# Spreading the weights' sums over a half, moving half of the operand rests to VectorE, and respacing the attention steps in a fused attention and FFN kernel

## The chip, the core and the metric

One core of a Trainium2 chip runs the kernel. The metric is the device time of one execution in microseconds (us). The time before is the median of three runs, 850.99 us (850.49 to 851.1). Five engines run side by side, each through its own instructions in program order: TensorE (PE; its weight loads are PEld), VectorE (DVE), ScalarE (ACT), GpSimd (POOL) and SyncE (SP), whose queue issues nearly all DMAs here.

## What is computed

Attention within chunks of 64 tokens (8 heads of 64 features), then a normalization, a feed-forward layer with ReLU, and the residual, all in fp32:

```python
scores = scale * np.matmul(q_c, k_c.transpose(0, 1, 2, 4, 3))   # chunks of 64 tokens
attn = np.exp(scores - np.max(scores, axis=-1, keepdims=True))
attn = attn / (np.sum(attn, axis=-1, keepdims=True) + 1e-09)
x = np.matmul(attn, v_c)                        # as (8 * 576 tokens, 512)
xn = (x - mean(x)) / np.sqrt(var(x) + 1e-06) * g_ln
out = x + np.maximum(xn @ w_ch1, 0.0) @ w_ch2   # 512 -> 2048 -> 512
```

## The kernel before

The 4608 tokens are 18 pairs of 128 (256 tokens each). To keep fp32 accuracy, every operand of the FFN is split in a high part (rounded on ScalarE, fp32r) and a rest (operand minus high part, on VectorE or GpSimd), and every product is three: high x high, high x rest, rest x high.

The first three tiles (six pairs) run in `START`, `SECOND` and `THIRD`, with an order written out by letters. They take the first 325 us of the profile, and the change does not touch them. The other 12 pairs are three **units** of four pairs (1024 tokens), `unit_ffn(u)` for u = 0, 1, 2. A unit has two stages:

- *Up*: the product with the first weights, in four quarters q. Seven products of sums of blocks take the place of eight products of blocks, so that a quarter has 14 steps of 6 matmuls (named "2", "1", "6", "5", "7", "3", "4"; L965). ScalarE copies banks out (L971), VectorE adds them (L974) into the tiles `h0` to `h7` (`hu`, L953 to L956; each holds two halves n of the tokens, two blocks f and 512 columns). The "4" product of a quarter goes into a bank that VectorE has first to read by the addition after "7".
- *Down*: for units 0 and 1, two halves n of 512 tokens, each 16 blocks f of 12 matmuls (L1092). Block f needs its high part (`split`, ScalarE, L1010) and its rest (`rest`, VectorE, L1015), which are issued two blocks ahead: the rest of block f + 2 after the eighth matmul of block f, and it is used from the eighth matmul of block f + 2 on, 24 matmuls later. Unit 2 (`tail`) has its own down stage (`double`, L891) in seven products as well; for this it needs sums of the second weights, in DRAM as `wb`.

Weights come through a ring of six places (`Ring`). After each block or each two up steps one more load is issued on SP's queue (L707 to L711).

Three things are done beside the matmuls of units 0 and 1:

- *Attention of the next unit's four pairs* (`following(u + 1, n)`), a generator of 20 steps: loads, scores (L302), maximum (L309), subtraction (L334), exp on ScalarE (L337), four steps of four transposes on VectorE (L362), row sums (L369), outputs (L391), scaling to x (L425), statistics (L435), xg (L447), its scaling on ScalarE (L453), one turn (L458), four steps of 4 row DMAs (L466).
- *`combine(u + 1, half)`*: the operands of the next unit's up stage from the rows of pairs 0 and 1 (half 0) or 2 and 3 (half 1): seven parts, each a high part on ScalarE (L773) and a rest on GpSimd (L774), and four subtractions on VectorE (L777).
- *`mix_weights(u)`*: for four p, the sums for `wb`: two sums of 512 columns out of the ring (L928), four of 256 (L935), a high part on ScalarE (L938), a rest on VectorE (L940), two DMAs (L942, L943). It is woven in by hand in the down stage of half n = 1: p = 0 to 3 in blocks 0 to 7 of unit 0, p = 4 to 7 in blocks 8 to 15 of unit 1. Its two buffers are the tiles `h0` and `h1`, in turn.

All is put in program order by `weave`: `unit_ffn` yields a cost, the number of its 512-column matmuls, and `side` is a list of (position, generator); a step is issued when the sum of the costs has come to its position. A unit has 720 positions: up 0 to 336, half n = 0 336 to 528, half n = 1 528 to 720. Pair n begins at position 114 n + 8, and its steps follow at the offsets of `STEPS`, scores at the first; `combine` has 11 steps, 9 positions apart, from 345 (half 0) and 515 (half 1). Steps are issued at the first yield at or after their position (every 6 positions in the up stage, every 4 in the blocks), and those with the same position in the order of the list.

Of the kernel before, what the change touches and what calls it, by code (L numbers as in the profile page):

```python
# [8 lines left out]
F32 = mybir.dt.float32  # L9
# [40 lines left out]

PAIR_SPAN = 114
LOADED = 8
STEPS = (0, 5, 9, 13, 18, 26, 34, 42, 50, 56, 62, 67, 76, 81, 87, 95, 104, 113, 122)
ONE_STEP = 9
FIRST_HALF = 345
LAST_HALF = 515
REST = (2, 6, 20)


# [41 lines left out]
def chunk_attention_ffn(ctx: ExitStack, tc: tile.TileContext, qkv, v01, g, w, out):  # L101
# [586 lines left out]
    class Ring:  # L688
# [22 lines left out]
                    nc.sync.dma_start(to.rearrange("p (h n) -> p h n", h=2), of)  # L711
                self.given += 1

        def peek(self, n):
            assert self.taken + n < self.given
            return self.places[(self.taken + n) % RING]

        def take(self):
            assert self.taken < self.given
# [35 lines left out]
    def operand(name):  # L755
        if name not in shared:
            shared[name] = const.tile([P, 2, 2, 2 * PAIR], F32R, name="xc", tag=f"w{'2165734'.index(name)}")
        return shared[name]

    def combine(u, half):  # L760
        cs = slice(half * PAIR, (half + 1) * PAIR)
        if u > 0:
            a, b = (
                r[:, half].rearrange("p j k t -> p (j k t)").rearrange("p (j k t) -> p k j t", k=NK, t=32)
                for r in shared["rows"]
            )
        else:
            a, b = (r[:, half].rearrange("p j k t -> p k j t") for r in shared["rows"])
        b11, b21, b12, b22 = a[:, :2], a[:, 2:], b[:, :2], b[:, 2:]

        def part(name, x):
            o = operand(name)[:, :, :, cs].rearrange("p h k (j t) -> p h k j t", t=32 if u > 0 else P)
            nc.scalar.copy(o[:, 0], x)  # L773
            nc.gpsimd.tensor_tensor(out=o[:, 1], in0=x, in1=o[:, 0].bitcast(F32), op=ALU.subtract)  # L774

        def less(out, x, y):
            nc.vector.tensor_tensor(out=out, in0=x, in1=y, op=ALU.subtract)  # L777

        part("2", b21)
        yield  # L780
        part("1", b11)
        yield
        less(b11, b12, b11)
        yield
        less(b12, b22, b12)
        yield
        part("3", b22)
        yield
        less(b22, b22, b11)
        yield  # L790
        part("6", b22)
        yield
        part("5", b11)
        yield
        less(b21, b21, b22)
        yield
        part("7", b12)
        yield
        part("4", b21)
        yield  # L800

    class double:

# [113 lines left out]
                    yield 3.17  # L917
                    self.advance(t + (k + 1) / 2)

    def mix_weights(u):  # L920
        for i in range(4):
            p = 4 * u + i
            space = shared[f"h{i % 2}"].rearrange("p n f d -> p (n f d)")
            t_ = space[:, : 2 * DM].rearrange("p (f d) -> p f d", f=2)
            his = space[:, 2 * DM :].bitcast(F32R).rearrange("p (f d) -> p f d", f=2)
            for k in range(2):
                w = ring.peek(k)[:, : 2 * DM].rearrange("p (h n) -> p h n", h=2).bitcast(F32)
                nc.vector.tensor_tensor(out=t_[:, k], in0=w[:, 0], in1=w[:, 1], op=ALU.add)  # L928
            yield
            b11, b12, b21, b22 = (t_[:, k // 2, k % 2 * PAIR : (k % 2 + 1) * PAIR] for k in range(4))  # L930
            for out, x, y, op in (
                (b11, b12, b11, ALU.subtract), (b12, b22, b12, ALU.subtract), (b22, b11, b22, ALU.subtract),
                (b21, b21, b22, ALU.add),
            ):
                nc.vector.tensor_tensor(out=out, in0=x, in1=y, op=op)  # L935
            yield
            yield
            nc.scalar.copy(his, t_)  # L938
            yield
            nc.vector.tensor_tensor(out=t_.bitcast(F32R), in0=t_, in1=his.bitcast(F32), op=ALU.subtract)  # L940
            yield
            nc.sync.dma_start(wb[:, p, 0], his.rearrange("p f (a n) -> p (f a) n", a=2).bitcast(F32))  # L942
            nc.sync.dma_start(wb[:, p, 1], t_.rearrange("p f (a n) -> p (f a) n", a=2))  # L943
            yield

    def unit_ffn(u):
        first = 2 * LEAD + 4 * u
# [138 lines left out]
        for n in range(2):  # L1086
            ys = [ps_y.tile([P, DM], F32, name="y") for _ in range(4 - 2 * n)]
            ys += [ps_h.tile([P, DM], F32, name="h") for _ in range(2 * n)]

            def down(f, w, j, m):  # L1090
                hh, hl = (x[:, j * P : (j + 1) * P] for x in parts[n * NF + f][:2])
                nc.tensor.matmul(  # L1092
                    ys[j], lhsT=(hh, hh, hl)[m], rhs=w[:, (0, 1, 0)[m]],
                    start=f == 0 and m == 0, stop=f == NF - 1 and m == 2,
                )

            pairs = [first + 2 * n, first + 2 * n + 1]
            early, late = ((2, 3, 0), 1) if n else ((0, 2, 1), 3)
            firsts = [(m, j) for m in range(2) for j in early] + [(0, late), (1, late)] + [(2, j) for j in (*early, late)]
            ws = {}  # L1100
            mixing = mix_weights(u) if n else iter(())
            for f in range(NF):
                if n and f >= 8 * u:
                    next(mixing, None)
                ws[f] = ring.take()[:, : 2 * DM].rearrange("p (h n) -> p h n", h=2)
                if f < NF - 2:
                    i = n * NF + f + ahead
                    for at, (m, j) in enumerate(
                        firsts if f == 0 else
                        [(m, j) for m in range(3) for j in range(4)]  # L1110
                    ):
                        down(f, ws[f], j, m)
                        if at % 4 == 3:
                            yield 4
                            if at == 11 and n == 0 and f == NF - 3:
                                split(NF)
                            if at == 3 and f > 0 and i - 1 < 2 * NF:
                                split(i - 1)
                            if at == 7 and f > 0 and i - 1 < 2 * NF:
                                rest(i - 1)  # L1120
                            if n and at < 8 and f >= 8 * u:
                                next(mixing, None)
                    ring.fetch()
                    if f == 6:
                        for pair in pairs:
                            back[pair] = unspill(pair)
                    for to, of in stores:
                        nc.sync.dma_start(to, of)
                    stores.clear()
            for j in range(4):  # L1130
                for f in range(NF - 2, NF):
                    for m in range(3):
                        down(f, ws[f], j, m)
                yield 6
                pair, jj = pairs[j // 2], j % 2
                x = back[pair][:, jj, :]
                nc.vector.tensor_tensor(out=x, in0=ys[j], in1=x, op=ALU.add)
                row = pair * PAIR + jj * P
                if tail and n == 1:
                    nc.sync.dma_start(out[row : row + P, :], x)  # L1140
                else:
                    stores.append((out[row : row + P, :], x))
                next(mixing, None)
# [54 lines left out]
    with tc.manual_schedule():  # L1198
# [19 lines left out]
        for u in range(UNITS):  # L1218
            side = [(at, now["Q"]) for at in REST] if u == 0 else []
            if u + 1 < UNITS:  # L1220
                for n in range(4):
                    begin = n * PAIR_SPAN + LOADED
                    side += [(begin + at, following(u + 1, n)) for at in STEPS]
                    side.append((begin + STEPS[0], following(u + 1, n + 1)))
                for half, begin in enumerate((FIRST_HALF, LAST_HALF)):
                    stream = combine(u + 1, half)
                    side += [(begin + i * ONE_STEP, stream) for i in range(11)]
            weave(unit_ffn(u), side)


# [33 lines left out]
```

## Time and profile before

| what | us |
|---|---|
| median of three runs | 850.99 |
| profiled execution, its time | 848.26 |
| profiled execution, its span (first to last instruction) | 846.5 |
| first part (tiles 0 to 2), from the chain | 0 to 324.75 |
| unit 0 (up 324.75 to 409.55, down to 507.59) | 182.84 |
| unit 1 (down from 592.39, to 686.03) | 178.44 |
| unit 2 (up to 762.19, down to 842.83) | 156.80 |

The starts are those of the merged pieces of the chain that ended last. Units 0 and 1 have the same matmuls. In the profile's groups a row reads: line, engine, operation, output <- inputs by the program's names, shape, count | busy us, mean ns of one | idle us of the engine before them, and what ended it. In the order of time: start, duration, engine, line, operation, count, and in brackets the idle time before it with what ended it. Instructions in a row on one engine are merged there.

### The profile page before, as it was taken

The numbers are of one execution on the slowest core, as the hardware profiler recorded it, in microseconds if no ns is written. First come the engines' busy times: TensorE is split into PE (matmuls) and PEld (weight loads), VectorE is DVE, ScalarE is ACT, GpSimd is POOL, SyncE is SP. The second block draws the span as 40 slices with busy tenths as digits, with TensorE's granted clock in tenths as the row PEclk, the third lists the DMA queues.
The fourth block names the chain that finished last, engine by engine and source line by source line (L and its number), as shares of the span: only waits on it lengthen the run. The fifth ranks groups of instructions, "written<-read, shape, count | busy, mean of one in ns | idle before, by whom it ended". The sixth has DMA issues, their size and how long they took to land.

```text
span 846.5 us, 15569 instructions
## 1 busy us (share of the span) xinstructions
PE 828.6 (98%) x6138; PEld 693.2 (82%) x6138; DVE 585.9 (69%) x961; ACT 298.3 (35%) x465; POOL 149.7 (18%) x138
## 2 busy tenths in 40 slices
PE   7999999999999999999999899999999999999998
PEld 4888888888888888878878688788788888889998
DVE  6999956777556736787795937679766653249854
ACT  5776432123331333232432312324333223245432
POOL 0110006474741133000231300000314000000000
PEclk9999999999999999999999999999999999999999
DMA  9997508937981138697787979778658897668672
GB/s 361 333 289 201 197 3 289 335 134 278 326 288 61 38 147 301 191 307 270 230 299 247 361 232 315 231 257 312 225 203 293 296 351 229 197 193 281 204 220 102
DMA packets 93113, 203.69 MB, mean 241 GB/s; under 512 B 9200, under 2 KB 47600, under 8 KB 91120
## 3 DMA queue, kind: packets, MB, share of 16 engines
q1 hardware_dynamic: 91744, 197.97, 67.7%
q0 software_dynamic: 1296, 4.72, 2.8%
q8 instruction: 49, 0.80, 0.4%
q14 instruction: 24, 0.20, 0.1%
HBM read 144.98 MB, written 48.76 MB: 229 GB/s over the span
## 4 chain that ended last, share of the span: by engine, by line
PE 90%; DVE 7%; DMA 1%; issue 1%; ACT 0%; SPq 0%; DVEq 0%
PE y L965 26%; PE h L547 16%; PE y L571 16%; PE y L1092 11%; PE y L891 10%; PE h L1092 4%; DVE pt_sb L362 2%; PE s L302 2%; PE h L391 1%; DVE hu L928 1%; DVE hx L1015 1%; PE s L391 1%; DMA k_t<-qkv 1%; DVE hu L935 1%; PE s L351 1%
## 5 line engine op out<-in xcount | busy, mean ns | idle before, releaser
L965 PE MATMUL y<-xc,ring 128*128 128x512 f32 x1008 | 233.2, 391 | 0.8 <-DVE hu L974 0.8
L965 PEld LDWEIGHTS y<-xc,ring 128*128 128x128 f32 x1008 | 188.2, 188 | 41.1 <-DVE hu L974 1.6
L547 PE MATMUL h<-xth,wp 128*128 128x512 f32 (+1 forms) x432 | 129.3, 370 | 0.0
L974 DVE TENSOR_TENSOR hu<-y,snap 128x512 f32<-128x512 f32 x72 | 49.1, 684 | 68.2 <-ACT snap L971 34.8
L571 PE MATMUL y<-wp,hh 128*128 128x512 f32 x376 | 96.2, 394 | 0.0
L547 PEld LDWEIGHTS h<-xth,wp 128*128 128x128 f32 x432 | 78.3, 188 | 14.0 <-DVE hl L561 0.2
L1092 PE MATMUL y<-ring,hx 128*128 128x512 f32 x324 | 84.5, 390 | 3.6 <-DVE hx L1015 3.6
L774 POOL TENSOR_TENSOR xc<-rows,xc 128x512 fp32r<-128x512 f32 x42 | 57.2, 1372 | 135.9 <-ACT xc L773 119.7
L362 DVE STREAM_TRANSPOSE pt_sb<-p_sb 32x256 f32<-32x256 f32 x176 | 76.7, 436 | 6.1 <-ACT p_sb L337 3.3
L571 PEld LDWEIGHTS y<-wp,hh 128*128 128x128 f32 x376 | 69.1, 188 | 13.9
L561 DVE SCALAR_TENSOR_TENSOR hl<-h,hh 128x512 fp32r<-128x512 f32 (+1 forms) x53 | 33.1, 629 | 65.4 <-ACT hh L560 65.1
L547 PE MATMUL h<-xtl,wp 128*128 128x512 f32 (+1 forms) x216 | 78.3, 367 | 0.0
L971 ACT COPY snap<-y 128x512 f32<-128x512 f32 x72 | 41.9, 585 | 101.5 <-PE y L965 101.3
L1092 PEld LDWEIGHTS y<-ring,hx 128*128 128x128 f32 x324 | 60.6, 188 | 17.1 <-DVE hx L1015 4.4
L560 ACT ACTIVATE hh<-h 128x512 fp32r<-128x512 f32 (+1 forms) x53 | 28.6, 546 | 117.7 <-PE h L547 117.7
L891 PE MATMUL y<-ring,hx 128*128 128x256 f32 x480 | 59.1, 283 | 0.0
L891 PEld LDWEIGHTS y<-ring,hx 128*128 128x128 f32 x480 | 58.2, 192 | 0.0
L571 PE MATMUL y<-wp,hl 128*128 128x512 f32 x188 | 51.8, 389 | 0.0
L1092 PE MATMUL y<-ring,hh 128*128 128x512 f32 x168 | 49.0, 407 | 0.0
L441 POOL TENSOR_TENSOR rstd<-vare,mhalf 128x2 f32<-128x2 f32 x12 | 10.5, 876 | 213.0 <-DVE vare L440 213.0
L547 PEld LDWEIGHTS h<-xtl,wp 128*128 128x128 f32 x216 | 40.3, 188 | 6.6 <-ACT xtl L510 0.2
L571 PEld LDWEIGHTS y<-wp,hl 128*128 128x128 f32 x188 | 35.3, 188 | 7.4
(153 smaller groups left out, 1149.9 us busy)
## 6 DMA issues: line engine op xcount, KB each, us to landing
ring<-wa SPq DMA_DIRECT2D x84, 512.0 KB, 4.5
ring<-w2d SPq DMA_DIRECT2D x64, 512.0 KB, 4.8
raw<-w SPq DMA_DIRECT2D x15, 1024.0 KB, 8.1
q_t<-qkv SPq DMA_DIRECT2D x17, 512.0 KB, 5.7
k_t<-qkv SPq DMA_DIRECT2D x17, 512.0 KB, 6.5
v_t<-qkv SPq DMA_DIRECT2D x32, 256.0 KB, 5.4
w2d<-wp SPq DMA_DIRECT2D x16, 512.0 KB, 7.6
wa<-parts SPq DMA_DIRECT2D x32, 256.0 KB, 4.6
```

Of the source, the lines that this page charges most:

```text
L302: nc.tensor.matmul(s[h2][c * D : (c + 1) * D, j * HP + a, :], lhsT=q_t[r, a, cs], rhs=k_t[r, a, cs], start=not den_by_pe or j == a == 0, s ...
L362: nc.vector.transpose(out=pt_sb[quad(2 * h2 + j), :, c, quad(i)], in_=p_sb[quad(2 * c + i), :, h2, quad(j)])
L547: nc.tensor.matmul(h, lhsT=(wh, wh, wl)[m][:, ks], rhs=(xth, xtl, xth)[m][:, k, :], start=i == 0, stop=i == len(terms) - 1,)
L560: nc.scalar.activation(hh, h, AF.Relu)
L561: nc.vector.scalar_tensor_tensor(out=hl, in0=h, scalar=0.0, in1=hh.bitcast(F32), op0=ALU.max, op1=ALU.subtract)
L571: nc.tensor.matmul(sums(pairs[j // 2])[j % 2], lhsT=(hh, hh, hl)[m], rhs=(wh, wl, wh)[m], start=f == 0 and m == 0, stop=f == NF - 1 and m ...
L774: nc.gpsimd.tensor_tensor(out=o[:, 1], in0=x, in1=o[:, 0].bitcast(F32), op=ALU.subtract)
L891: nc.tensor.matmul(bank[j // 2][:, j % 2 * PAIR : (j % 2 + 1) * PAIR], lhsT=(hh, hh, hl)[m][:, j * P : (j + 1) * P], rhs=loaded[t // 2][:, ...
L965: nc.tensor.matmul(bank, lhsT=w[:, (0, 0, 1)[m], ks], rhs=x[:, (0, 1, 0)[m], k, :], start=start and k == m == 0, stop=k == 1 and m == 2, s ...
L971: nc.scalar.copy(out, bank)
L974: nc.vector.tensor_tensor(out=out, in0=bank, in1=s, op=ALU.add)
L1092: nc.tensor.matmul(ys[j], lhsT=(hh, hh, hl)[m], rhs=w[:, (0, 1, 0)[m]], start=f == 0 and m == 0, stop=f == NF - 1 and m == 2,)
```

## The change

- `mix_weights(u, i)` takes one p of four at a time, in side steps: for i = 0 to 3, eight steps at 528 + 48 i + `MIXING`, so that one p falls to every four blocks of half n = 1, in both units. Unit u takes p = 2 i + u, whose weights are blocks 4 i + 2 u and 4 i + 2 u + 1 of the half. It reads them out of the ring by number (`ring.at`), in unit 1 two and three blocks ahead of the block under way. Its buffers are the n = 0 halves of `h{2i}` and `h{2i + 1}`, other ones for each i. The rest of 1024 columns becomes two of 512.
- `combine` of units 1 and 2 has 13 steps, and a rest is issued one or more steps after its high part. The rests of half 1 are on VectorE; those of half 0 stay on GpSimd. Half 0 runs from 426 with 8 positions between steps, half 1 from 562 with 12.
- `STEPS` has new offsets: the transposes are 11 positions apart (8 before), the outputs 67 behind the scores (56 before), with the later steps behind them. Pair 2 (n = 2) has its own offsets, `ACROSS`: xg and all that follows come 25 positions later than in `STEPS`, so that nothing of the pair falls between positions 313 and 346.

The order for unit 0's own operands (`combine(0, ...)`) keeps its 11 steps. The diff, without the deletion of the old loop's hooks in `unit_ffn` (`next(mixing, None)` in four places) and without the old list of `combine`, whose order stays in the `else` branch:

```diff
-STEPS = (0, 5, 9, 13, 18, 26, 34, 42, 50, 56, 62, 67, 76, 81, 87, 95, 104, 113, 122)
-ONE_STEP = 9
-FIRST_HALF = 345
-LAST_HALF = 515
+STEPS = (0, 5, 9, 14, 20, 31, 42, 53, 61, 67, 72, 77, 85, 90, 97, 104, 111, 118, 125)
+ACROSS = (0, 5, 9, 14, 20, 31, 42, 53, 61, 67, 72, 77, 110, 116, 123, 130, 136, 142, 148)
+HALVES = ((426, 8), (562, 12))
+SECOND_HALF = 528
+MIXING = (1, 4, 13, 16, 24, 37, 41, 47)
...
-        def peek(self, n):
-            assert self.taken + n < self.given
-            return self.places[(self.taken + n) % RING]
+        def at(self, i):
+            assert self.taken - 1 <= i < self.given
+            return self.places[i % RING]
...
+        engine = nc.vector if u > 0 and half == 1 else nc.gpsimd
+
+        def cast(name, x):
+            nc.scalar.copy(place(name)[:, 0], x)
+
+        def low(name, x):
+            o = place(name)
+            engine.tensor_tensor(out=o[:, 1], in0=x, in1=o[:, 0].bitcast(F32), op=ALU.subtract)
...
+        if u > 0:
+            steps = [
+                [(cast, "2", b21)], [(low, "2", b21), (cast, "1", b11)], [(low, "1", b11), (cast, "3", b22)],
+                [(less, b11, b12, b11)], [(low, "3", b22)], [(less, b12, b22, b12)], [(less, b22, b22, b11)],
+                [(cast, "6", b22), (cast, "5", b11)], [(low, "6", b22)], [(less, b21, b21, b22), (cast, "7", b12)],
+                [(low, "5", b11)], [(cast, "4", b21), (low, "7", b12)], [(low, "4", b21)],
+            ]
...
-    def mix_weights(u):
-        for i in range(4):
-            p = 4 * u + i
-            space = shared[f"h{i % 2}"].rearrange("p n f d -> p (n f d)")
-            t_ = space[:, : 2 * DM].rearrange("p (f d) -> p f d", f=2)
-            his = space[:, 2 * DM :].bitcast(F32R).rearrange("p (f d) -> p f d", f=2)
...
+    def mix_weights(u, i):
+        p = 2 * i + u
+        t_ = shared[f"h{2 * i}"][:, 0]
+        his = shared[f"h{2 * i + 1}"][:, 0].bitcast(F32R)
+        for k in range(2):
+            w = ring.at(ring.passed + 2 * p + k)[:, : 2 * DM].rearrange("p (h n) -> p h n", h=2).bitcast(F32)
+            nc.vector.tensor_tensor(out=t_[:, k], in0=w[:, 0], in1=w[:, 1], op=ALU.add)
+            yield
...
+            nc.vector.tensor_tensor(out=out, in0=x, in1=y, op=op)
+            if k % 2:
+                yield
+        nc.scalar.copy(his, t_)
+        yield
+        for k in range(2):
+            nc.vector.tensor_tensor(
+                out=t_[:, k].bitcast(F32R), in0=t_[:, k], in1=his[:, k].bitcast(F32), op=ALU.subtract
+            )
+            yield
+        nc.sync.dma_start(wb[:, p, 0], his.rearrange("p f (a n) -> p (f a) n", a=2).bitcast(F32))
+        nc.sync.dma_start(wb[:, p, 1], t_.rearrange("p f (a n) -> p (f a) n", a=2))
+        yield
...
-                    side += [(begin + at, following(u + 1, n)) for at in STEPS]
+                    side += [(begin + at, following(u + 1, n)) for at in (ACROSS if n == 2 else STEPS)]
                     side.append((begin + STEPS[0], following(u + 1, n + 1)))
-                for half, begin in enumerate((FIRST_HALF, LAST_HALF)):
+                for half, (begin, step) in enumerate(HALVES):
                     stream = combine(u + 1, half)
-                    side += [(begin + i * ONE_STEP, stream) for i in range(11)]
+                    side += [(begin + i * step, stream) for i in range(13)]
+                for i in range(NF // 4):
+                    stream = mix_weights(u, i)
+                    side += [(SECOND_HALF + 12 * i * 4 + at, stream) for at in MIXING]
```

More of the change, by code (lines that the diff above doesn't have):

```diff
@@ L769, in combine, with place, part @@
         b11, b21, b12, b22 = a[:, :2], a[:, 2:], b[:, :2], b[:, 2:]
[L771 to L774, printed above, removed]
+        def place(name):
+            return operand(name)[:, :, :, cs].rearrange("p h k (j t) -> p h k j t", t=32 if u > 0 else P)
+        engine = nc.vector if u > 0 and half == 1 else nc.gpsimd
[4 more added lines that the diff above has]
+            engine.tensor_tensor(out=o[:, 1], in0=x, in1=o[:, 0].bitcast(F32), op=ALU.subtract)
         def less(out, x, y):
             nc.vector.tensor_tensor(out=out, in0=x, in1=y, op=ALU.subtract)
[L779 to L800, printed above, removed]
+        def part(name, x):
+            cast(name, x)
+            low(name, x)
+        if u > 0:
[5 more added lines that the diff above has]
+            ]
+        else:
+            steps = [
+                [(part, "2", b21)], [(part, "1", b11)], [(less, b11, b12, b11)], [(less, b12, b22, b12)],
+                [(part, "3", b22)], [(less, b22, b22, b11)], [(part, "6", b22)], [(part, "5", b11)],
+                [(less, b21, b21, b22)], [(part, "7", b12)], [(part, "4", b21)],
+            ]
+        for step in steps:
+            for what, *args in step:
+                what(*args)
+            yield
     class double:
@@ L918, in products @@
                     self.advance(t + (k + 1) / 2)
-    def mix_weights(u):
-        for i in range(4):
-            p = 4 * u + i
-            space = shared[f"h{i % 2}"].rearrange("p n f d -> p (n f d)")
-            t_ = space[:, : 2 * DM].rearrange("p (f d) -> p f d", f=2)
-            his = space[:, 2 * DM :].bitcast(F32R).rearrange("p (f d) -> p f d", f=2)
-            for k in range(2):
-                w = ring.peek(k)[:, : 2 * DM].rearrange("p (h n) -> p h n", h=2).bitcast(F32)
-                nc.vector.tensor_tensor(out=t_[:, k], in0=w[:, 0], in1=w[:, 1], op=ALU.add)
-            yield
[L930 to L935, printed above, removed]
-            yield
[L937 to L944, printed above, removed]
@@ new lines, in mix_weights @@
+    def mix_weights(u, i):
[5 more added lines that the diff above has]
+            nc.vector.tensor_tensor(out=t_[:, k], in0=w[:, 0], in1=w[:, 1], op=ALU.add)
+            yield
+        b11, b12, b21, b22 = (t_[:, k // 2, k % 2 * PAIR : (k % 2 + 1) * PAIR] for k in range(4))
+        for k, (out, x, y, op) in enumerate((
+            (b11, b12, b11, ALU.subtract), (b12, b22, b12, ALU.subtract), (b22, b11, b22, ALU.subtract),
+            (b21, b21, b22, ALU.add),
+        )):
+            nc.vector.tensor_tensor(out=out, in0=x, in1=y, op=op)
[7 more added lines that the diff above has]
+            )
+            yield
+        nc.sync.dma_start(wb[:, p, 0], his.rearrange("p f (a n) -> p (f a) n", a=2).bitcast(F32))
+        nc.sync.dma_start(wb[:, p, 1], t_.rearrange("p f (a n) -> p (f a) n", a=2))
+        yield
@@ L1100, in unit_ffn @@
             ws = {}
-            mixing = mix_weights(u) if n else iter(())
+            ring.passed = ring.taken
             for f in range(NF):
-                if n and f >= 8 * u:
-                    next(mixing, None)
                 ws[f] = ring.take()[:, : 2 * DM].rearrange("p (h n) -> p h n", h=2)
@@ L1120, in unit_ffn @@
                                 rest(i - 1)
-                            if n and at < 8 and f >= 8 * u:
-                                next(mixing, None)
                     ring.fetch()
@@ L1142, in unit_ffn @@
                     stores.append((out[row : row + P, :], x))
-                next(mixing, None)
                 if n == 0 and j < 3:
```

## The prediction, made before the changed kernel was timed

> **What bounds it now.** I read the page first: its busy line, then the stretches of 30 us, the waits, the clock, and last the order of time at each wait.
>
> ```profile
> span 846.5 us, 15569 instructions
> PE 828.6 (98%) x6138; PEld 693.2 (82%) x6138; DVE 585.9 (69%) x961; ACT 298.3 (35%) x465; POOL 149.7 (18%) x138
> ```
>
> TensorE sets the end. All the diff's code runs in units 0 and 1 of the second part, so I ask what TensorE loses there. The chain in order of time gives the rate (start, us, what):
>
> ```profile
> 409.55 2.73 PE y L1092 x12
> ...
> 510.31 1.09 PE s L302 x64
> ...
> 686.03 76.16 PE y L965 x336
> 762.19 80.64 PE y L891 x672
> ```
>
> 336 matmuls in 76.16 us are 0.2267 us each: one position of `weave`. Unit 2 (from 686 us) runs at that rate without a gap, so nothing is to be had there. A block of 12 is 2.72 us. An attention step on TensorE (64 small matmuls) costs 1.09 us, about 1.3 with the change-over.
>
> Units 0 and 1 by stretches (PE, PEld, DVE, ACT, POOL busy; clock; DMA share; GB/s), and all waits of TensorE's matmuls for VectorE there:
>
> ```profile
> 420.00:450.00 30.00, 28.31 (x182) 23.16 (x181) 24.42 (x41) 10.55 (x19) 7.86 (x6) 1.00 0.77 275
> 450.00:480.00 30.00, 28.62 (x126) 23.22 (x125) 25.48 (x38) 10.14 (x17) 7.81 (x6) 1.00 0.87 320
> 480.00:510.00 30.00, 27.79 (x115) 22.23 (x113) 13.80 (x19) 4.95 (x9) 2.65 (x2) 0.94 0.79 264
> ...
> 600.00:630.00 30.00, 28.26 (x175) 23.00 (x174) 26.78 (x46) 11.68 (x20) 7.83 (x6) 0.94 0.68 243
> ```
>
> ```profile
> PE y L1092 <- DVE hx L1015: 3.6, 2, 2.2
> PE h L391 <- DVE pt_sb L362: 3.4, 4, 1.2
> PE y L965 <- DVE hu L974: 0.8, 2, 0.4
> ```
>
> Sum: 3.6 + 3.4 + 0.8 = **7.8 us of waits, all for VectorE**: 1.7, 1.4, 2.2 and 1.7 us idle in the four stretches, and 0.8 in two up stages. Two stretches have clock 0.94; in steps of 3 us:
>
> ```profile
> 429.00:432.00 3.00, 2.57 (x65) 2.25 (x66) 2.90 (x6) 1.78 (x4) 2.24 (x2) 1.00 0.90 362
> ...
> 486.00:489.00 3.00, 3.00 (x11) 2.17 (x10) 2.92 (x4) 2.66 (x6) 0.00 (x0) 0.69 0.98 400
> 489.00:492.00 3.00, 3.00 (x11) 2.41 (x10) 1.96 (x4) 0.63 (x1) 0.00 (x0) 0.74 0.98 300
> ...
> 612.00:615.00 3.00, 2.67 (x62) 2.32 (x63) 2.90 (x6) 1.68 (x4) 2.14 (x2) 0.74 0.60 238
> 615.00:618.00 3.00, 3.00 (x11) 2.41 (x10) 2.96 (x7) 0.00 (x0) 0.00 (x0) 0.69 0.28 116
> ```
>
> Each dip costs 3 x 0.31 + 3 x 0.26 = 1.7 us and stands right behind a wait (2.2 us; 1.7 us); the wait before 429 us had none. Two dips: **3.4 us**. So 7.8 + 3.4 = **11.2 us** can go at most by this list.
>
> **The change, part by part.** (a) *Weights' sums over 16 blocks.* In order of time at the two waits of the second half, unit 0:
>
> ```profile
> 458.66 1.29 DVE L928 TENSOR_TENSOR hu<-ring 128x512 f32<-128x512 f32 x2
> ...
> 472.77 2.38 DVE L928 TENSOR_TENSOR hu<-ring 128x512 f32<-128x512 f32 x2
> ...
> 477.52 0.73 PE L1092 MATMUL y<-ring,hx 128*128 128x512 f32 x2 [1.38 <-DVE hx L1015]
> ...
> 479.13 3.52 POOL L774 TENSOR_TENSOR xc<-rows,xc 128x512 fp32r<-128x512 f32 x2 [5.13 <-ACT xc L773]
> ...
> 479.73 3.48 DVE L928 TENSOR_TENSOR hu<-ring 128x512 f32<-128x512 f32 x2
> ...
> 485.58 0.73 PE L1092 MATMUL y<-ring,hx 128*128 128x512 f32 x2 [2.21 <-DVE hx L1015]
> ```
>
> The same two sums take 1.29 us alone and 3.48 beside GpSimd's rests (L774). The durations:
>
> ```profile
> L774 POOL TENSOR_TENSOR xc<-rows,xc 128x512 fp32r<-128x512 f32 x42 | 57.2, 1372 | 135.9 <-ACT xc L773 119.7 <-DMA rows<-x 10.1 <-DMA ring<-w2d 4.1
> ...
> L856 DVE TENSOR_TENSOR hx<-hu,hx 128x512 fp32r<-128x512 f32 x34 | 23.0, 686 | 7.9 <-ACT hx L847 7.7
> ...
> L1010 ACT ACTIVATE hh<-hu 128x512 fp32r<-128x512 f32 x28 | 17.3, 627 | 16.9 <-PE h L1092 8.8 <-PE y L1092 8.1
> ...
> L935 DVE TENSOR_TENSOR hu<-hu 128x256 f32<-128x256 f32 x32 | 13.5, 423 | 0.8
> ...
> L940 DVE TENSOR_TENSOR hu<-hu 128x1024 fp32r<-128x1024 f32 x8 | 9.8, 1222 | 2.4 <-ACT hu L938 2.4
> ```
>
> One p costs VectorE 1.29 + 4 x 0.423 + 1.22 = 4.2 us. Now, four p in 8 blocks (21.8 us of TensorE): 16.8 + 8 rests x 0.69 = 5.5 + 4 subtractions x 0.69 = 2.8, that is 25.1 us, 3.3 too many; the waits there are 3.6. After, one p in 48 positions (10.9 us): 4.2 + 4 rests 2.8 + (b) four steps of `combine` with at most one VectorE operation each, 2.8, that is 9.8 us, 90%. A rest is issued 24 positions (5.4 us) ahead of its matmuls, so 1.1 us to spare per 48 is enough: 3.6 us and the first dip go. In unit 1, where the sums now stand in the last 8 blocks without a wait, the same 90% hold throughout.
>
> (b) *Second half's rests on VectorE.* 7 x 0.69 = 4.8 us more on VectorE per unit (a low like L856, two SBUF operands, is the nearest row), counted above; it takes 7 GpSimd operations of 1.37 us out, each of which can hold VectorE up (3.48 - 1.29 = 2.2 us for two). Without that cover (no GpSimd overlap avoided), it would cost 4.8 us of an engine that then has 1.1 us to spare per 48 positions, and nothing on the path.
>
> (c) *Pair steps.* Four transposes are one step; the fourth, and who waits for it:
>
> ```profile
> 427.56 1.81 DVE L362 STREAM_TRANSPOSE pt_sb<-p_sb 32x256 f32<-32x256 f32 x4
> ...
> 428.60 0.29 PE L391 MATMUL h<-v_t,pt_sb 64*64 64x64 f32 x2 [1.15 <-DVE pt_sb L362]
> ...
> 429.43 1.14 PE L391 MATMUL h<-v_t,pt_sb 64*64 64x64 f32 x58 [0.54 <-DVE pt_sb L362]
> ...
> 440.81 1.84 DVE L1015 SCALAR_TENSOR_TENSOR hl<-hu,hh 128x512 fp32r<-128x512 f32 x2
> ```
>
> The steps stand 8 positions apart, 1.81 us for 1.8 us of work: VectorE has no room for rests and `combine` between. After, they are 11 apart (2.5 us), the outputs' matmuls come 70 instead of 56 positions after the scores, and `combine` of the first half starts at 426, behind them. In the up stage this frees VectorE for the additions that TensorE waits for at L974 (0.8 us). In the first half, pair 2's two last VectorE steps now come in (moved past the stages' change):
>
> ```profile
> L447 DVE SCALAR_TENSOR_TENSOR xg<-x,mv,g_sb 128x512 f32<-128x512 f32 x36 | 28.1, 823 | 0.0
> ...
> L309 DVE TENSOR_REDUCE top<-s 128x16 f32<-128x1024 f32 x18 | 22.0, 1220 | 18.2 <-PE s L302 18.1
> L334 DVE TENSOR_TENSOR p_sb<-s,top 128x1024 f32<-128x1024 f32 x16 | 19.5, 1219 | 0.4
> ...
> L337 ACT ACTIVATE p_sb<-p_sb 128x1024 f32<-128x1024 f32 x16 | 16.9, 1058 | 25.9 <-DVE p_sb L334 25.9
> ...
> L458 DVE STREAM_TRANSPOSE x<-xg 128x1024 f32<-128x1024 f32 x8 | 9.9, 1242 | 4.6 <-ACT xg L453 4.6
> ```
>
> VectorE's order after, from the half's first matmul: xg 2 x 0.82, done in the gap ahead of the scores; scores (position 352) end at 16 x 0.2267 + 1.1 = 4.7; top 5.9; a rest 6.6; pair 2's turn 7.9; subtraction 9.1; exp 10.2 on ScalarE; the split queued behind it 10.8; its rest, first in VectorE's queue, 11.5; three transposes' steps with a rest between 17.5; a rest 18.2; the fourth step 20.0. The outputs (position 420) are due at 84 x 0.2267 + 1.3 = 20.3. Now the fourth step ends at 429.37 - 409.55 = 19.8 and is due 1.7 us earlier. So the wait falls from 1.7 to between 0 and 0.9 (one GpSimd hold-up); I take 0.3 per unit, as the tally is the nearest number. Behind it, the stretch from the fourth step's end to the rests of blocks 10 and 11 takes 440.81 - 429.37 = 11.4 us now; after, one rest, one subtraction and the turn (0.7 + 0.7 + 1.2) are no longer ahead of block 10's, so it ends at 20.0 + 11.4 - 2.6 + 0.7 = 29.5, due at position 464 (29.0 + 2.6 = 31.6). The 2.1 us between cover one GpSimd hold-up, not two: 0 to 0.9, I take 0.1. Pair 2's statistics now stand at 318, just ahead of the addition that the "4" product at 330 needs: 0 to 0.3, I take 0.1.
>
> (d) *Queues.* The row DMAs of pairs move by up to 35 positions on SP's queue, with the ring's fetches behind them; a fetch has five blocks (13.6 us) from its issue slot to its use. One of a pair's four steps of row DMAs on SP:
>
> ```profile
> 363.86 2.51 SPq L466 DMA_DIRECT2D rows<-x  x4
> ```
>
> All four take 10 us, so a fetch behind them is up to 7 us late and lands 4.5 us later (median; the ring's row stands with the rivals): 2 us to spare, taken as nothing, 0 to 1 per unit. The sums' stores wait for VectorE at the head of SP's queue, with the next fetch behind: same cover. Own buffers take away the wait of a sum for the store two p before; TensorE does not wait for it now.
>
> Sum: -7.8 - 3.4 + 2 x (0.3 + 0.1 + 0.1) = -10.2 us. 848.26 - 10.2 = 838.1 in a profiled execution; its time stands 2.73 below the median of the runs, 850.99, so **840.8 us**.
>
> The dips I take as caused by the waits, because both stand behind the longest idle stretches. [...]
>
> **Rivals.** *First half still bound by the pair* (18%): ScalarE's order (split behind exp) or GpSimd's rests keep the outputs' wait at 1.7 us and unit 1's dip. Gain 3.6 + 1.7 + 0.8 = 6.1: 844.9 us. For: VectorE has no idle time from 9 to 32 us of the half by my tally. Against: 14 positions (3.2 us) more before the outputs.
>
> *Dips stay* (8%): they come on their own clock, not from waits; against it stands that unit 2 has none. Gain 6.8: 844.2 us. [...]
>
> *The load only moves* (8%): the second half at 90% in both units waits about as much as now, since in-order hold-ups (his copy, stores) eat the 1.1 us. Unit 1 then pays what unit 0 pays (3.6 + 1.7), unit 0 keeps it; the pair's part still gains 5.1 or less: about 850 to 851 us.
>
> *Slower: sums wait for loads* (6%). In unit 1 the sums read blocks two and three ahead, whose loads were issued 28 positions (6.3 us) before:
>
> ```profile
> DMA to landing us min/median/max: 3.3/4.5/8.8
> ```
>
> At 8.8 us, or behind a late SP queue, VectorE stands still and everything behind it, rests included. A hold-up of h per p costs TensorE h - 1.1 once the 5.4 us of lead are used. Over 8 p the 11.2 us gain is gone at h = 2.5, and it is slower by 0.2% at 2.7; at h = 4 it is 8 x 2.9 - 10.2 = +13: 864 us. Against: the median leaves 1.8 us, and unit 0 reads loaded blocks.
>
> **Numbers.** Forecast 840.8, 58%, own range 839.3 to 843.3. With the first two rivals and 2% for a still larger gain, 86% faster by over 0.2% (1.7 us, about what a measurement of this kernel can tell from no change), 8% within, 6% slower. The range 839.0 to 846.5 leaves out the last two rivals and the rim.
>
> **What would show it.** Right: no wait of L1092 for L1015 in the second half, clock 1.00 in every stretch after 420 us, the outputs' wait (L391 for L362) under 0.5 us, TensorE idle under 1.5 us in units 0 and 1, VectorE near 90% in the second half of both. Wrong: a new wait at L965 near the stages' change, at L1092 around blocks 10 and 11, VectorE idle for ring loads, or a dip without a wait before it.

## The result, and the profile after

The changed kernel takes 836.38 us (median of 4 runs, 835.88 to 836.6) against 850.74 us for the kernel before (4 runs, 850.4 to 851.1): a ratio of 0.983, 95% interval 0.9813 to 0.9847. That is 14.4 us faster where 10.2 us were forecast, and it lies below the range, whose low end was 839.0 us.

The page's first lines after, then all waits of TensorE's matmuls in the whole execution (line, what it waited for, us in total, times, longest):

```profile
span 834.5 us, 15570 instructions
## 1 busy us (share of the span) xinstructions
PE 823.5 (99%) x6138; PEld 690.4 (83%) x6138; DVE 590.4 (71%) x983; ACT 298.1 (36%) x465; POOL 133.1 (16%) x124
```

```profile
PE y L243 <- ACT minus L1202: 2.4, 1, 2.4
PE s L303 <- DMA k_t<-qkv: 1.5, 1, 1.5
PE s L303 <- ACT p_sb L333: 1.1, 1, 1.1
PE y L243 <- DVE x L412: 0.7, 1, 0.7
PE h L548 <- DMA wp<-wf: 0.7, 1, 0.7
PE s L392 <- issue: 0.3, 1, 0.3
PE s L303 <- PE y L501: 0.3, 1, 0.3
PE h L548 <- DVE hl L562: 0.3, 1, 0.3
```

All eight belong to the first part. Of the 7.8 us of waits in units 0 and 1 nothing is left: neither L1100 (down stages), nor L973 (up stages), nor a pair's outputs after 326 us stands in the list. The stretches of 30 us that were shown before, now:

```profile
420.00:450.00 30.00, 30.00 (x192) 24.72 (x191) 27.28 (x45) 13.02 (x24) 9.53 (x7) 1.00 0.74 251
450.00:480.00 30.00, 30.00 (x133) 24.64 (x133) 25.53 (x45) 10.70 (x19) 2.35 (x2) 1.00 0.88 320
480.00:510.00 30.00, 30.00 (x193) 24.69 (x192) 18.59 (x31) 8.24 (x13) 0.00 (x0) 1.00 0.96 340
...
600.00:630.00 30.00, 30.00 (x192) 24.72 (x191) 26.93 (x41) 9.54 (x18) 11.85 (x8) 1.00 0.68 227
```

TensorE is busy throughout and its clock is 1.00. VectorE works 27, 26, 19 and 27 us of 30 in these stretches, against 24, 25, 14 and 27 before: no less, and yet it is not waited for.

The best measure of all that follows is the length of a stage: from the start of its first matmul to that of the next stage, in the order of time. The work on TensorE is the same in all kernels, so a longer stage is lost time. Each length is from one profiled execution. In us, with the median of the runs (the kernel before, executed beside them, had medians of 849.4 to 850.7):

| kernel | up 0 | down 0 | up 1 | down 1 | median |
|---|---|---|---|---|---|
| before | 84.79 | 98.05 | 84.80 | 93.64 | 850.74 |
| before, once more | 84.77 | 97.86 | 84.78 | 93.68 | 850.42 |
| **changed** | 84.11 | 89.82 | 84.10 | 89.68 | 836.38 |
| old_sums | 84.10 | 92.02 | 84.12 | 89.68 | 837.74 |
| old_sums_own | 84.12 | 91.04 | 84.10 | 89.68 | 836.67 |
| old_steps | 84.79 | 89.71 | 84.79 | 89.69 | 838.30 |
| gpsimd_rests | 84.12 | 90.02 | 84.11 | 91.13 | 837.51 |
| combine_alone | 84.77 | 89.84 | 84.82 | 89.69 | 837.03 |
| combine_gpsimd | 84.80 | 92.45 | 84.78 | 90.41 | 840.83 |
| vector_second | 84.79 | 96.31 | 84.80 | 92.08 | 846.91 |
| late_first | 84.77 | 95.57 | 84.77 | 89.92 | 842.18 |
| sums_alone | 84.79 | 91.97 | 84.79 | 93.56 | 843.75 |
| steps_alone | 84.12 | 95.88 | 84.07 | 90.63 | 843.35 |

Unit 2's up stage is 76.16 us in every row. Units 0 and 1 together went from 361.28 to 347.71 us: **13.6 us**. No kernel has a shorter up stage than 84.1 us or a shorter down stage than 89.7, so the changed kernel stands at this floor to within 0.1 us, and no other beat it in these stages. (Single executions also differ in the first part: those of gpsimd_rests go from 834.89 to 838.64 us with a mean clock of 1.000 in all.)

Some lengths hold a *dip*, a stretch in which TensorE's granted clock stands at 0.50 (for 3.41 us in the kernel before, last section) and 1.7 us are lost: both down stages of both profiles of the kernel before, down 0 of late_first and down 1 of sums_alone. No other row has one in units 0 and 1. Which wait is followed by a dip varies (last section), so 1.7 us come off these lengths before kernels are compared by their waits.

### The profile page after: what moved, and what is told of

Read it like the earlier page. It is cut to its first block, busy times and chain, and to the rows that moved or that the text cites. A ratio compares the mean times of both kernels' runs of the same rounds, so it can differ in the third digit from the quotient of the medians.

```text
span 834.5 us, 15570 instructions
## 1 busy us (share of the span) xinstructions
PE 823.5 (99%) x6138; PEld 690.4 (83%) x6138; DVE 590.4 (71%) x983; ACT 298.1 (36%) x465; POOL 133.1 (16%) x124
## 4 chain that ended last, share of the span: by engine, by line
PE 95%; DMA 2%; DVE 1%; ACT 1%; issue 0%; SPq 0%; DVEq 0%
PE y L973 28%; PE y L1100 16%; PE h L548 15%; PE y L572 15%; PE y L898 10%; PE h L1100 5%; PE s L303 2%; PE h L392 1%; DMA wp<-wf 1%; DMA k_t<-qkv 1%; PE s L392 1%; PE s L352 1%; PE s L329 0%; PE y L243 0%; PE s L480 0%
## 5 line engine op out<-in xcount | busy, mean ns | idle before, releaser
L973 PE MATMUL y<-xc,ring 128*128 128x512 f32 x1008 | 232.6, 391 | 0.0
L973 PEld LDWEIGHTS y<-xc,ring 128*128 128x128 f32 x1008 | 188.2, 188 | 39.7
L1100 PE MATMUL y<-ring,hx 128*128 128x512 f32 x324 | 84.5, 390 | 0.0
L1100 PEld LDWEIGHTS y<-ring,hx 128*128 128x128 f32 x324 | 60.6, 188 | 12.9 <-issue 0.3
L782 POOL TENSOR_TENSOR xc<-rows,xc 128x512 fp32r<-128x512 f32 x28 | 39.7, 1436 | 48.7 <-ACT xc L778 48.5
L1100 PE MATMUL y<-ring,hh 128*128 128x512 f32 x168 | 46.5, 390 | 0.0
```

Of the source, the lines that this page charges most:

```text
L782: engine.tensor_tensor(out=o[:, 1], in0=x, in1=o[:, 0].bitcast(F32), op=ALU.subtract)
L973: nc.tensor.matmul(bank, lhsT=w[:, (0, 0, 1)[m], ks], rhs=x[:, (0, 1, 0)[m], k, :], start=start and k == m == 0, stop=k == 1 and m == 2, s ...
L1100: nc.tensor.matmul(ys[j], lhsT=(hh, hh, hl)[m], rhs=w[:, (0, 1, 0)[m]], start=f == 0 and m == 0, stop=f == NF - 1 and m == 2,)
```

## The experiments

**The kernel before, once more.** No edit.

> The kernel before once more, unchanged. Theory W (TensorE's waits for VectorE and the clock dips behind them are the whole gain): the same eight waits in units 0 and 1, 7.8 us in all (give or take 0.3), units 0 and 1 together 361 to 364 us long against 347.7 us in the changed kernel; the 2.5 us by which the profiled execution lay under the other runs is a dip that a wait has in one execution and not in another (1.7 us a dip). Theory D (the dips and the first part vary by themselves, waits or not): dips also where no wait stands before them, or the 2.5 us in the first 325 us.

The waits came back to the tenth, and units 0 and 1 took 361.1 us. Two things vary between executions. The first part took 324.59 us in the first profile of the kernel before (to the first matmul of unit 0), and 325.0 to 327.3 us in all later profiles of all kernels. Most of the difference is one wait in the first part, for converted weights that a DMA brings; in this kernel's own list, and in that of old_sums_own:

```profile
PE h L547 <- DMA wp<-wfs: 0.9, 1, 0.9
```

```profile
PE h L548 <- DMA wp<-wfs: 2.4, 1, 2.4
```

The first profile of the kernel before had no such wait, nor had those of old_sums and vector_second (325.1 and 325.0 us). The other thing is the clock: over the runs of the kernel before, the mean clock goes from 0.992 (853.7 us) to 0.999 (846.7 us), while the changed kernel has 1.000 in all four of its runs. One dip takes 1.7 us of some 850 at full clock, 0.002 of the mean; the step from 0.999 to 0.992 is three or four dips, 5 to 7 us (an estimate). So neither theory was wholly right: no dip stands without a wait before it, but not every wait has one, and part of the 2.5 us lay in the first part.

**The old sums in the changed kernel, and the same with buffers of their own.**

```diff
-            ring.passed = ring.taken
+            mixing = mix_weights(u) if n else iter(())
             for f in range(NF):
+                if n and f >= 8 * u:
+                    next(mixing, None)
...
-                for i in range(NF // 4):
-                    stream = mix_weights(u, i)
-                    side += [(SECOND_HALF + 12 * i * 4 + at, stream) for at in MIXING]
```

> The changed kernel with the old mix_weights: four p in eight blocks, buffers h0 and h1. Theory W (overload of VectorE by the sums): waits at L1100 are back in unit 0's second half, 3 to 4 us with one dip, so unit 0 about 5 to 6 us longer; in unit 1 the sums now meet the end of the combination, 0 to 4 us. Time 841 to 847 us. Rival L (the overload came only from GpSimd holding VectorE up, and the second half has no GpSimd rests any more): no waits, 836 to 837.5 us.

Between the two: two waits of 1.5 us in unit 0, no dip, 2.2 us of stage. The order of time in unit 0 (old_sums) shows a cause that neither named:

```profile
470.90 1.29 DVE L935 TENSOR_TENSOR hu<-ring 128x512 f32<-128x512 f32 x2 [1.43 <-DMA wb<-hu]
...
474.56 0.73 PE L1099 MATMUL y<-ring,hx 128*128 128x512 f32 x2 [0.88 <-DVE hx L1022]
```

VectorE, without which TensorE cannot go on, stood 1.43 us until the store of the sum two before had left the shared buffer. Hence the second kernel, old_sums with the changed kernel's buffers:

```diff
-            space = shared[f"h{i % 2}"].rearrange("p n f d -> p (n f d)")
+            t_ = shared[f"h{2 * i}"][:, 0]
+            his = shared[f"h{2 * i + 1}"][:, 0].bitcast(F32R)
```

> old_sums with one edit: buffers of their own for each of the four sums (h0 to h7, the n = 0 halves), still four p in eight blocks. In old_sums VectorE stood 1.4 us for the store of the sum two before, and TensorE's two waits (1.5 us) came after it. Theory B (the shared buffers' store wait is what is left of the overload): no wait at L1100 over 0.3 us in unit 0, down stage 89.7 to 90.1 us (92.0 in old_sums), time as the changed kernel. Rival (four p in eight blocks are too many): 1 to 1.5 us of waits stay, down stage 91.3 to 92 us.

One wait of 0.6 us is left and the stage is 1.2 us over the changed kernel's: the buffers bring 1.0 of the 2.2 us. Both expectations missed it, one on either side. The remaining 1.2 us are not shown to be the crowding's alone: here VectorE stood still for a load of the ring at the first p's sums, long before the wait:

```profile
460.43 0.69 DVE L934 TENSOR_TENSOR hu<-ring 128x512 f32<-128x512 f32 x1 [1.37 <-DMA ring<-w2d]
...
482.29 0.73 PE L1098 MATMUL y<-ring,hx 128*128 128x512 f32 x2 [0.63 <-DVE hx L1021]
```

This is the mechanism of the slower rival, sums that wait for loads. And combine_alone (below) has the four sums in the same eight blocks, with the old shared buffers, and no wait in its down stages. Its first down stage begins within 0.1 us of this one's, and the sums of its third p at 470.95 us, 1.2 us earlier than here (472.16), since no load and no store held them up.

**The old offsets of the pairs in the changed kernel**, and the new ones (with `ACROSS`) alone in the kernel before, by the reverse of this edit.

```diff
-STEPS = (0, 5, 9, 14, 20, 31, 42, 53, 61, 67, 72, 77, 85, 90, 97, 104, 111, 118, 125)
+STEPS = (0, 5, 9, 13, 18, 26, 34, 42, 50, 56, 62, 67, 76, 81, 87, 95, 104, 113, 122)
...
-                    side += [(begin + at, following(u + 1, n)) for at in (ACROSS if n == 2 else STEPS)]
+                    side += [(begin + at, following(u + 1, n)) for at in STEPS]
```

> The changed kernel with the old offsets of all pairs (no ACROSS either). Theory W (transposes 8 positions apart leave VectorE no room): the outputs' wait of 1 to 1.7 us in each of units 0 and 1, and 0.4 us at L982 in each up stage, with or without a dip: 2 to 4 us per unit, 840 to 844 us. Rival C (the wait came from the combination of half 0 between the transposes, which now begins at 426): outputs' wait under 0.3 us, only the up stages' 0.7 us per unit come back, 837.5 to 838.5 us.

Theory C holds. The outputs do not wait; only the up stages are 0.68 us longer, each for one wait of 0.4 us at the addition:

```profile
PE y L973 <- DVE hu L982: 0.8, 2, 0.4
```

> The kernel before with nothing but the new pair offsets (STEPS and ACROSS). All theories: up stages 84.1 us (84.8 before), unit 0's second half as before. Theory C (the combination between the transposes makes the outputs' wait): it still stands between them here, so L391 waits 0.5 to 1.7 us in both first halves; time 846 to 849.5 us. Rival S (the spacing alone ends the wait): under 0.3 us there, down stages 95.8 and 89.7 us, time 842 to 844.5 us.

With the combination still between the transposes, the new offsets cut the outputs' wait from 1.7 to 0.4 us per unit (the second row); the second half's waits stay (the first):

```profile
PE y L1093 <- DVE hx L1016: 3.8, 2, 2.2
...
PE h L392 <- DVE pt_sb L363: 0.8, 2, 0.4
```

C's wait was 0.5 to 1.7, S's under 0.3: the measured 0.4 lies between. The time is S's, but in part by luck: this profile has no dip, though the second half waits 2.2 us as before. Less the dip of the kernel before (98.05 - 1.7 = 96.3), unit 0's down stage fell by 0.5 us only, unit 1's by 1.3.

**Half 0 of the combination begins at 426**, alone, in the kernel before.

```diff
-                for half, begin in enumerate((FIRST_HALF, LAST_HALF)):
+                for half, (begin, step) in enumerate(((426, 8), (LAST_HALF, ONE_STEP))):
```

> The kernel before with nothing but half 0 of the combination moved from 345 (9 apart) to 426 (8 apart), old steps, old second half. Theory C (the combination between the transposes makes the outputs' wait): no outputs' wait over 0.5 us in both units, unit 1's down stage 89.7 us (93.6 before); unit 0's second half as before, so its down stage 94.5 to 96.5 us (98 before); up stages 84.8. Rival: the outputs' wait stays 1.7 us.

As theory C has it. The list of waits has no row for the outputs, unit 1's down stage falls by 3.7 us (1.7 of it the dip), and the second half of unit 0 waits 3.6 us as ever. This one edit is worth about 6 us in units 0 and 1. What of the combination made the wait, its subtractions among VectorE's transposes or GpSimd's rests beside them, the run does not tell apart.

**The new combine alone in the kernel before** (the list of 13 steps, rests of half 1 on VectorE, `HALVES`), and the same with those rests back on GpSimd.

```diff
-FIRST_HALF = 345
-LAST_HALF = 515
+HALVES = ((426, 8), (562, 12))
...
+        engine = nc.vector if u > 0 and half == 1 else nc.gpsimd
...
+                [(cast, "2", b21)], [(low, "2", b21), (cast, "1", b11)], [(low, "1", b11), (cast, "3", b22)],
...
```

> The kernel before with nothing but the new combine (half 0 from 426, half 1 from 562 with its rests on VectorE); old sums, old pair offsets. Theory C (the outputs waited because the combination stood between the transposes; a wait costs its row plus 0.3 us, and a dip): no wait of L391/L392 for the transposes over 0.3 us in the first halves; the up stages stay 84.8 us; unit 0's second half keeps about 1.5 us of waits as in old_sums. Down stages 92.0 and 89.7 us (98 and 93.6 before), time 838.5 to 841 us. Rival S (the pair's new offsets are needed as well): outputs' waits of 0.5 to 1.7 us stay, 842 to 846 us.

Theory C holds, and more: no wait is left in unit 0's second half either, where 1.5 us were expected, though all four sums stand in its first eight blocks with buffers shared. Down stages of 89.84 and 89.69 us are the changed kernel's.

```diff
-        engine = nc.vector if u > 0 and half == 1 else nc.gpsimd
+        engine = nc.gpsimd
```

> combine_alone (the kernel before with the new combine) with the second half's rests back on GpSimd at the new positions, beside the old sums. Theory L (GpSimd's rests hold the sums up; that, on top of a full VectorE, made unit 0's waits): waits at L1097 of 1 to 3.5 us are back in unit 0's second half, its down stage 91 to 95 us (89.8 in combine_alone); unit 1 89.7 to 91 us. Rival P (only the position of the combination counted): no wait over 0.3 us, 89.7 to 90.0 us in both.

Theory L holds: 2.3 us of waits are back. The sums beside a GpSimd rest, in this kernel's order of time, and the same line in the groups of both kernels (mean ns; combine_gpsimd, then combine_alone):

```profile
458.71 1.28 DVE L933 TENSOR_TENSOR hu<-ring 128x512 f32<-128x512 f32 x2
...
470.97 2.98 POOL L780 TENSOR_TENSOR xc<-rows,xc 128x512 fp32r<-128x512 f32 x2 [5.13 <-ACT xc L776]
472.74 2.38 DVE L933 TENSOR_TENSOR hu<-ring 128x512 f32<-128x512 f32 x2
...
477.48 0.73 PE L1097 MATMUL y<-ring,hx 128*128 128x512 f32 x2 [1.29 <-DVE hx L1020]
```

```profile
L933 DVE TENSOR_TENSOR hu<-ring 128x512 f32<-128x512 f32 x16 | 14.7, 956 | 3.0 <-DMA wb<-hu 3.0
```

```profile
L933 DVE TENSOR_TENSOR hu<-ring 128x512 f32<-128x512 f32 x16 | 10.3, 685 | 4.8 <-DMA wb<-hu 4.8
```

The two sums take 2.38 us in place of 1.28, with the second rest of GpSimd on until 473.95, and they end 1.17 us after that, about their time alone. By what GpSimd holds them up, these rows do not show.

**GpSimd for the second half's rests in the changed kernel** (the same edit there).

> The changed kernel with the second half's rests back on GpSimd, at the new positions. Theory W (the load of the sums decides, the engine of the rests does not): no wait or under 0.5 us, 836 to 837.5 us. Rival L (GpSimd's hold-ups of VectorE made the waits): 1 to 3 us of waits at L1100 in each second half, 838.5 to 843 us.

Between the theories: unit 0 stays as it was (90.02 us), unit 1 has one wait of 1.2 us. With the sums spread, GpSimd's hold-ups cost 1.7 us over both units, in place of 3.3 (92.45 + 90.41 against 89.84 + 89.69) with the sums in eight blocks.

**VectorE for the second half's rests in the kernel before**, at about the old positions (begin, distance and number of steps per half; half 0 keeps its old steps).

```diff
+HALVES = ((345, 9, 11), (515, 7, 13))
...
+        engine = nc.vector if u > 0 and half == 1 else nc.gpsimd
...
+        if u > 0 and half == 1:
+            steps = [
+                [(cast, "2", b21)], [(low, "2", b21), (cast, "1", b11)], [(low, "1", b11), (cast, "3", b22)],
...
```

> The kernel before with nothing but the second half's rests on VectorE, in the 13 new steps, at about the old positions (515, 7 apart: 515 to 599); old sums, old first half, old offsets. Theory L (hold-ups by GpSimd): the second half's waits shrink from 3.6 to under 1.5 us though VectorE has 4.8 us more to do in the same blocks; unit 0's down stage 92 to 95 us (98 before). Theory O (plain overload, as the prediction had it: 25.1 us of work in 21.8 us): 4.8 us more make it worse, 5 to 8 us of waits, down stage 99 to 103 us. The outputs' waits of 1.7 us stay in both units by either.

Theory O's forecast falls: with 4.8 us more on VectorE about the same blocks the waits of the second half do not grow. By their rows they shrink, from 3.6 to 2.9 us (1.8 for VectorE, 1.1 for ScalarE's high parts, which are new), but they are more in number, and the stage is no shorter: 96.31 us without a dip, against 98.05 - 1.7 = 96.3. Unit 1's 1.6 us, too, are its missing dip. Theory L's under 1.5 us of waits and its 92 to 95 us were too good. No GpSimd operation stands in its order of time from 458 to 478 us, and VectorE works nearly without a pause, so the waits for VectorE that are left look like plain load.

**The new sums alone in the kernel before.**

> The kernel before with nothing but the new mix_weights. Theory of the overload: the two waits of unit 0's second half go with their dip, about 6 us; the outputs' waits (1.7 us each in both units) and the up stages' stay; time 842.5 to 845 us. Rival L (GpSimd's rests, still in the second half here and now beside sums in both units, hold VectorE up): 1 to 2.5 us of waits at L1092 in each unit, 845 to 850 us.

The second half's waits go altogether, with GpSimd's rests still there (its sums take 930 ns in the mean); the first row of this kernel's list is the outputs' wait that stays:

```profile
PE h L393 <- DVE pt_sb L364: 3.4, 4, 1.2
```

Unit 0's down stage falls by 6.1 us (1.7 of it the dip), as the overload theory had it; the edit spreads the sums and gives them buffers of their own at once. So the waits of the second half go in two ways: by the new sums, or by the combination moved to 562 with its rests off GpSimd. Of the latter neither part is enough: moved alone, 2.3 us of waits stay (combine_gpsimd); off GpSimd alone, 2.9 (vector_second). The gains do not add: 6.1 (sums_alone) and 8.2 (combine_alone, which ends the outputs' wait as well) together give 8.2.

**What a wait costs, and what makes a dip.** In unit 2's up stage of the changed kernel, the addition after the second "7" is repeated:

```diff
+REPEATS = (6, 7, 8, 10)
...
+                for _ in range(REPEATS[q] if tail and e else 1):
+                    add(h[e][:, 1, 1], a_[e], s[e][2])
```

> The changed kernel, in whose unit 2 (no side work, no wait) the addition after the second 7 product is done 6, 7, 8 and 10 times over in quarters 0 to 3 of the up stage, with the same result each time, so that TensorE waits for it ahead of the second 4 product: about 1.4, 2.1, 2.8 and 4.2 us (repeats x 0.69 less 2.7 of lead), each costing its row plus 0.3 us. Theory W (dips come from waits as short as those of the kernel before): the granted clock falls below 0.9 within 4 us behind two or more of the waits under 3.4 us, each such dip costs about 1.7 us. [...] The up stage is 76.2 + 11.7 = 87.9 us without dips.

The four waits in the order of time, and the granted clock (the number before the last two) in the steps of 3 us behind them:

```profile
693.12 7.10 PE L974 MATMUL y<-xc,ring 128*128 128x512 f32 x30 [1.76 <-DVE hu L983]
...
714.95 1.60 PE L974 MATMUL y<-xc,ring 128*128 128x512 f32 x3 [2.48 <-DVE hu L983]
...
739.10 1.22 PE L974 MATMUL y<-xc,ring 128*128 128x512 f32 x2 [3.21 <-DVE hu L983]
...
765.01 2.93 PE L974 MATMUL y<-xc,ring 128*128 128x512 f32 x6 [5.03 <-DVE hu L983]
```

```profile
693.00:696.00 3.00, 2.88 (x13) 2.38 (x14) 0.66 (x2) 1.23 (x2) 0.00 (x0) 1.00 0.20 30
...
714.00:717.00 3.00, 2.06 (x5) 1.67 (x6) 1.45 (x3) 0.63 (x1) 0.00 (x0) 0.67 0.03 11
717.00:720.00 3.00, 3.00 (x11) 2.36 (x11) 0.00 (x0) 0.60 (x1) 0.00 (x0) 0.76 0.30 75
...
738.00:741.00 3.00, 1.90 (x5) 1.51 (x6) 1.61 (x3) 0.63 (x1) 0.00 (x0) 0.65 0.02 5
741.00:744.00 3.00, 3.00 (x12) 2.40 (x11) 0.00 (x0) 0.60 (x1) 0.00 (x0) 0.78 0.31 48
```

Theory W holds: dips behind 2.48 and 3.21 us (and one that begins within the 5.03 us wait: the clock reads 0.64, 0.50 and 0.73 in the steps from 762 to 771 us), none behind 1.76. The stage took 94.21 us, 18.05 more than without: 12.5 of waits by the rows, 4 x 0.3 beside them, and 4.4 left for three dips, the last of which runs past the stage's end (from there to the end of the span it is 85.30 us in place of 84.46). The waits were 0.4 to 0.8 us longer than expected, so 76.2 + 11.7 was too little.

## Why the prediction was wrong in size and right in kind

- *TensorE's waits for VectorE are the whole gain*: right, all eight went.
- **The term that failed is that of the waits: 7.8 us.** The row of a matmul's wait counts from the modelled end of the matmul before, 0.39 us behind its start (391 ns in the mean of L965 before), while behind a matmul without a wait the next one begins after 0.227 (76.16 / 336): that is half of it. And the second matmul behind a wait begins 0.34 us after the first, in place of 0.227 (the two at 485.58 take 0.73 us, less 0.39). An up stage whose one wait is 0.38 us by that row is 84.79 - 84.11 = 0.68 us longer. So each wait costs 0.3 us more than its row, eight waits 10.2 us. With 3.4 us for the two dips this is 13.6, the measured 13.6 of units 0 and 1. By unit 0's down stage: 1.15 + 0.54 + 1.38 + 2.21 + 4 x 0.3 + 1.7 = 8.2; measured 98.05 - 89.82 = 8.2. The other down stages come out to 0.3 us in this way, except steps_alone's first, which is 1.1 us longer than so worked out; that stays open.
- *New waits of 1.0 us*: there were none. The tally of VectorE's queue, worked out from rows, was close where it could be compared. The fourth step of transposes was to end 20.0 us into the first half, the outputs to be due at 20.3. In the order of time of the changed kernel, whose first half begins at 410.24:

```profile
428.39 1.81 DVE L363 STREAM_TRANSPOSE pt_sb<-p_sb 32x256 f32<-32x256 f32 x4
...
430.69 1.16 PE L392 MATMUL h<-v_t,pt_sb 64*64 64x64 f32 x64
```

  that is 19.96 and 20.45. The allowance for GpSimd's hold-ups behind it was not used.
- *The profiled execution stands 2.73 us below the median, after as before*: wrong. After, it stands 0.14 below (836.24). The 2.73 us were a first part without its DMA wait (1.5 us shorter than in the changed kernel's profile), and most likely one dip less than other runs had; dips go with the waits, so this offset was partly a gain. That last share is argued from the mean clock of the runs (0.993 in the slowest of before_again, 0.996 in its profile with two dips); no trace of a run with three dips exists.
- The forecast's 840.8 and the measured 836.4 differ by 4.4: 2.4 (waits' price) + 1.0 (new waits) + 2.6 (offset) - 1.5 (first part) = 4.5. The price of a wait alone would have put the forecast at 838.4.
- *(a) Overload of VectorE by the sums, 25.1 us in 21.8*: too simple. Spreading ends the waits, as forecast (sums_alone), but the same blocks with 25.7 us of work by the same tally (the old sums beside five combination operations) ran without a wait in combine_alone. An excess of 3.9 us over 21.8 is less than the lead of 24 positions, 5.4 us, and the lead takes it up as long as GpSimd does not hold VectorE up and no store or load is waited for. In vector_second, with ten such operations, the tally is 29.2 us (an estimate), 7.4 over, and TensorE waits. The agreement of 3.3 with 3.6 us was chance.
- *(b) Moving rests to VectorE costs nothing*: right, and underrated. In combine_alone it is worth 3.3 us, though it adds 4.8 us to the busier engine; at the old positions it gains nothing (vector_second).
- *(c) Spacing and a later combination end the outputs' wait*: right, but the prediction did not say which. The combination out from between the transposes is enough (late_first, old_steps); the spacing alone brings the wait to 0.4 us. The spacing's own share beside the new combine is the up stages' 2 x 0.68 us (old_steps).
- *(d) Queues*: right. Own buffers were put at nothing, and brought 1.0 us in old_sums_own, where the sums are crowded; combine_alone did without them.
- *The slower rival, sums that wait for loads*: it occurs, and decides nothing. VectorE's row for it in the changed kernel:

```profile
DVE hu L933 <- DMA ring<-w2d: 8.5, 7, 2.2
```

  The longest hold-up, 2.2 us, is under the 2.5 us that the rival needed at every one of eight sums. Crowded sums have less room for it (old_sums_own).
- *The clock dips stay*: refuted, the clock of the changed kernel reads 1.00 in units 0 to 2 throughout. The rival had a point in that the falls seem to keep to a grid of time (an estimate, last section), but each of the falls in units 0 to 2 of these profiles stands at a wait.

## What to carry to other kernels

A wait in a profile can cost the engine more than its row (here 0.68 us for 0.38); compare whole stages of equal work, and take a stage that runs without a gap as the floor. Where several edits reach the same wait, find by single edits which are enough: here moving and re-homing the operands' combination alone (837.0 us) came within 1.4 us of units 0 and 1 of the full change. Before shifting work off a busy engine, look whether the idle engine's work holds the busy one up: with room for it, VectorE got faster by taking more on (combine_alone against combine_gpsimd: 685 ns for a sum in place of 956, and 837.0 us in place of 840.8).

## What was not expected of the hardware

The granted clock fell behind idle stretches of TensorE as short as 2.2 to 2.5 us, and in unit 1 behind two within 1 us, of 1.20 and 0.54 us. In steps of 3 us it reads 0.65 to 0.78, but that is a mixture: cut where the clock changes, the kernel before has (PE busy in the second column, the clock third from the end):

```profile
483.73:487.14 3.41, 1.56 (x6) 1.14 (x7) 2.79 (x5) 2.14 (x4) 0.00 (x0) 1.00 0.99 384
487.14:490.55 3.41, 3.41 (x9) 2.68 (x9) 3.17 (x6) 2.03 (x4) 0.00 (x0) 0.50 1.01 351
...
610.02:613.43 3.41, 1.67 (x66) 1.36 (x65) 3.29 (x7) 2.97 (x6) 2.27 (x2) 1.00 0.93 366
613.43:616.84 3.41, 3.41 (x9) 2.74 (x9) 3.34 (x7) 0.25 (x1) 0.71 (x1) 0.50 0.15 59
```

So the clock stood at 0.50 for 3.41 us each time, which costs 1.7 us. How these falls lie in time can only be estimated. The two are 126.29 us apart, and a third, with TensorE's work done (the clock reads 1.00 up to 845.50 us, 0.68 in the next 0.1 us, then 0.50), begins at about 845.54, 232.1 us behind the second: 37 and 68 times 3.413 us. In repeats the clock in the steps of 3 us puts the first two falls at about 715.0 and 738.9, 23.9 us apart, or 7 times 3.413; the third, worked out in the same way, lasts about 6.8 us, twice as long.

In the 3.41 us ahead of the two falls of the kernel before, TensorE was busy for 1.56 and 1.67 us. How much idle time makes the clock fall was not shown, and the length of the waits does not tell it alone: steps_alone waits 2.20 us with no dip behind it, where the kernel before waits 2.21 with one, and in unit 1 vector_second waits 1.21 and 0.54 us without a dip, where the kernel before waits 1.20 and 0.54 with one. That like waits lie otherwise in such a grid is the author's estimate; it fits the spread of the kernel before from run to run (846.7 to 853.7 us).
